# Seven products for eight pairs in GEMM2, in two groups, with a reordered convolution

## The chip, the core and the metric

One core of a Trainium2 chip runs the kernel. The metric is device time in microseconds. The kernel before was run three times: 1254.81, 1254.21 and 1253.92, median 1254.21. One more execution was profiled. Engine names as in the profile: PE is TensorE, PEld its weight loads, DVE VectorE, ACT ScalarE, POOL GpSimd, SP the queue that issues most DMAs.

## What is computed

With x = A_q (2048 x 1024) and xn its layer norm over the last axis, the output is x + A + B:

```python
# A: convolution branch
for t in range(ks):                       # ks = 4
    k_shift = k_shift + k_pad[:, t:t + S, :] * shift_k[:, ks - 1 - t]
kv = k_shift * v
y = irfft(rfft(kv, 2S) * rfft(ssm_k, 2S))[:S] + kv * ssm_D
A = xn * y
# B: feed-forward branch
h = silu(xn @ w1)                         # 2048 x 3584
B = h @ w2                                # 2048 x 1024
```

All is float32. The kernel forms each product of matrices from float16 parts (hi and lo of both operands, three matmuls: hi hi, hi lo, lo hi).

## The kernel before, in words

**Planner.** The program is written out once by a planner (`Order`, L118). Every strand of work is a generator (a stream) that yields either an operation with an engine and an expected cost, or a condition (a `Token` or a free buffer). The planner always emits the operation that could start first, less the stream's bias (`add(gen, bias)`). What it emits is each engine's queue, and a queue runs strictly in order on the chip. So a flag orders what is emitted; the real waits follow from data and buffers.

**GEMM1.** F = 3584 is 28 blocks of 128, which are 14 pairs. Pairs 0 and 1 partly run plain; the others take seven products instead of eight for a 2 x 2 blocking (`PRODUCTS`, L50): the factors of w1 and x are hi and lo splits of sums (`factors_w1`, `x_rows`, `more_sums`). `units` (L993) runs `P1, P7, P6, P2, P5, (next P1), P3, P4` per pair and row half `sp`; `evacuate` (L909) turns PSUM banks (tile ff) into h through SiLU.

**From h to GEMM2.** A pair that is not in `PAIRS` is split into hi and lo and stored plain (`blocks`, L871: one split of 1024 columns per pair and quarter). A pair in `PAIRS` = (8, 9, 10, 11) goes to `quad` (L828), which makes the seven left factors of GEMM2: splits of (A11, A12), A22, (S3, S1) and (S2, S4), and four sums, stored in the DRAM tiles `hsf`. `split` (L370) is always a ScalarE copy to hi and a VectorE subtraction (L352) to lo.

**GEMM2.** `feed_forward` (L1057) first runs the 20 plain blocks (`PLAIN`) as five chunks of four, for column half 1 (h = 0) and then half 0, over 16 row tiles; `result` stores each tile. Then `units2` (L1118) runs the seven products of the four pairs for eight tile quadruples u, each with four output tiles; `evacuate2` (L1184) adds two of them on VectorE (`v_stt`) and sends all to `out` by accumulating DMAs on POOL (`G`, L344). The last unit waits for the flag "conv out", reads one tile back and stores it plainly.

**Factors of w2.** `norms_w2` (L1304) fills eight places of 8 KB a partition (`places`, tile x in the profile, which held x in GEMM1). Plain chunks go to `W2PLACE`; the seven right factors and a float32 `hold` go to `FPLACE` as the chunks leave. Raw w2 comes through four half slots (wraw, w2n), in 36 loads for the seven products (`RAWS`, `load_w2`).

**Convolution.** Eight channel groups g, each a two-stage transform on VectorE with DFT matmuls on TensorE. Per group: `gate` (taps and product with v into sig), `signal_parts` (cm, transposes by DMA), `stage1` (DFT matmuls into ps banks; i = 0 gives a half, i = 1 adds the rest), `to_spec` (L1589: ScalarE copies twice the half into "diff" and the sum into "total", VectorE subtracts), `forward`, `product`, `inverse`, `result_parts` (splits into zh, zl), `stage1_inv` (L1753, into py banks), `gated` (multiplies with xg, writes to out). Quarters are taken in the order `TO` = (1, 3, 0, 2). Diffs of odd quarters lie in tmp, those of even ones in spec. The flag "taken" says that `result_parts` of the group before has read a quarter's slot. When GEMM1 has ended, `spare` (L1586) lets stage 1 use ff banks too. Conv outputs of groups 0 to 3 are plain stores on SP, those of 4 to 7 accumulate on POOL.

Of the kernel before, what the change touches and what calls it, by code (L numbers as in the profile page):

```python
# [20 lines left out]
P = 128  # L21
# [32 lines left out]
PAIRS = (8, 9, 10, 11)  # L54
UNITS = [[*range(2, NP)], [NP - 1, 0, 1, *range(2, NP - 1)]]
NQ = len(PAIRS)
# [7 lines left out]
RAWS = {"B11": [(0, 0)], "B21": [(1, 0)], "B22": [(1, 1)], "T1": [(0, 1), (0, 0)], "T2": [(0, 0)],  # L64
        "T3": [(1, 1), (0, 1)], "T4": [(1, 0)]}
# [235 lines left out]
def h3_ffn_kernel(ctx, tc, x, kp, vs, fs, shift, dskip, w1, w2, cfwd, cinv, out):  # L301
# [77 lines left out]
    hsf = [{p[0]: dram.tile([4, P, NQ, 2, P], F16, name=f"hsf{p[0]}{b}") for p in PRODUCTS.values()} for b in range(2)]  # L379
# [448 lines left out]
    def quad(i, sp):  # L828

        def factors(names, hf, toks=()):  # L830
# [4 lines left out]
            for f, name in enumerate(names):  # L835
                yield L(hsf[sp][name][:, :, PAIRS.index(i)].rearrange("q p h s -> p q (h s)"),
                        ht[:, 4 * f:4 * f + 4].rearrange("p q h s -> p q (h s)"))
                ttok.set()
# [18 lines left out]
    for sp in range(2):  # L857
        flag["quads", sp] = Token(NQ)

# [197 lines left out]
    def feed_forward():  # L1057
# [13 lines left out]
        for h in range(2):  # L1071
            for ts in TOGETHER[h]:
                pos = {}
                for c in range(NC):
                    for t in ts:
                        if c == 0:
                            yield ff.ready
                            pos[t] = ff.tile([P, W])
                        yield flag["h", h, t, c]
                        hx, htok = flag["h", h, t, c].what  # L1080
                        yield flag["w2", h, c]
                        wc, wtok = w2c[h, c]
                        yield from steps2(pos[t][0], hx, wc, c == 0, c == NC - 1)
                        htok.set()
                        if t == NT - 1:
                            wtok.set()
                        if c == NC - 1:
                            add(result(h, t, *pos[t]), EB)
        flag["last part"].set()
        yield from units2()  # L1090


    TOGETHER = ([range(3)] + [(t,) for t in range(3, NT)],
                [(t,) for t in range(NT - 3)] + [range(NT - 3, NT)])

    def steps2(po, hx, wc, first, last, more=False):
        for n in range(4):
            def mm(n=n):
# [3 lines left out]
                nc.tensor.matmul(po, hx[:, n, 1, :], wc[:, n, 0, :], start=False, stop=last and n == 3, **kw)  # L1102
# [15 lines left out]
    def units2():  # L1118

        def product2(n, u, o, first=False, cols=slice(0, W), end=True):  # L1120
            yield flag["h2", u, n]
            hx, htok = flag["h2", u, n].what
            yield flag["w2f", n]
            wc, wtok = w2f[n]
            yield from steps2(o[:, cols], hx, wc[:, :, :, cols], first, True, not first)
            if end:
                htok.set()
                if u == len(tiles2) - 1:
                    wtok.set()

        def start(u):
# [4 lines left out]
            add(evacuate2(u, one, made, seen), EB)  # L1136
# [3 lines left out]
        for u in range(len(tiles2)):  # L1140
# [23 lines left out]
            if u + 1 < len(tiles2):  # L1164
# [5 lines left out]
            if u + 1 < len(tiles2):  # L1170
# [6 lines left out]

    def at(u, r, h):

        sp, q = tiles2[u]  # L1180
        t = 4 * (2 * sp + r) + q
        return orr[t // T2, t % T2, :, h * W:(h + 1) * W]

    def evacuate2(u, one, made, seen):  # L1184

        last = u == len(tiles2) - 1
# [5 lines left out]
        def copied(src, tok, to):  # L1192
# [3 lines left out]
            yield G(to, o)  # L1196
# [16 lines left out]
        if not last:  # L1213
            yield made["P2"]
            add(copied(*one, at(u, 0, 0)), EB)
# [7 lines left out]
        if last:  # L1223
            yield made["P2"]
            add(copied(*one, at(u, 0, 0)), EB)
        yield G(at(u, 1, 1), d)
# [5 lines left out]
        add(copied(two, k2, at(u, 0, 1)), EB)  # L1232
        if not last:
# [3 lines left out]
            yield G(at(u, 1, 0), a)  # L1237
# [11 lines left out]
    for n in range(NT):  # L1249
        flag["conv row", n] = Token(NG // 2)  # L1250

    def columns(h):

        return slice((1 - h) * W, (2 - h) * W)

    def result(h, t, po, tok):
# [4 lines left out]
        to = orr[t // T2, t % T2, :, columns(h)]  # L1261
        if h == 0:
            yield L(to, o)
            flag["row", t].set()
        else:
            yield flag["conv row", t]
            yield G(to, o)
        otok.set()

    def load_h():  # L1270
        yield flag["factors"]
        for h in range(2):
            for c, t in [(c, t) for ts in TOGETHER[h] for c in range(NC) for t in ts]:
# [4 lines left out]
        for u, n in uses2():  # L1278
            sp, q = tiles2[u]
            yield wo.ready  # L1280
            flag["h2", u, n].what = o, _ = wo.tile([P, NQ, 2, P], F16)
            yield L(o, hsf[sp][PRODUCTS[n][0]][q])
            flag["h2", u, n].set()
# [20 lines left out]
    def norms_w2():  # L1304
# [17 lines left out]
        add(load_w2(), 0.05)  # L1322
        for h in range(2):
            for c in range(NC):
                r = places[W2PLACE[h][c]]
                yield r.ready
                if (h, c) == (0, 0):
                    yield flag["x", 1, "A22"]
                wc, wtok = w2c[h, c] = r.tile([P, 4, 2, W], F16)
                flag["w2", h, c].n = 2  # L1330
                for a in (0, 2):
# [586 lines left out]
```

## Time and profile before

| | us |
|---|---|
| median of the runs | 1254.21 |
| profiled execution, device time | 1252.18 |
| its span, first to last instruction | 1250.1 |
| PE busy | 1235.8 |
| DVE busy | 1108.4 |
| ACT busy | 779.5 |
| mean granted TensorE clock | 0.995 |

The span is what the profile's stretches and timelines are measured in; around it lie 2.1 us of the profiled execution. Matmuls overlap, so a busy PE says only that one was in flight; the distance from one start to the next is what a matmul takes. The same holds, less strongly, for DVE, whose instructions overlap by some 0.08 us at their ends. In rows of waits, "A <- B: 25.8, 20, 3.6" means that A was idle 25.8 us in total in 20 waits ended by B, the longest 3.6.

### The profile page before, as it was taken

To read this page: it belongs to the slowest core of one execution; us is meant where nothing else is said; L and a number is where in the kernel's file an instruction comes from. 1 tells how busy PE (TensorE), PEld (TensorE's weight loads), DVE (VectorE), ACT (ScalarE), POOL (GpSimd) and SP (SyncE) were. 2 spreads that over 40 slices of the span, in tenths; PEclk is the share of its full clock that TensorE was granted. 3 is DMA by queue.
4 is the path that set the end of the run, shared out by engine and by line. 5 is a ranking of instruction groups with operands and counts; after the bars stand their busy time and mean duration, and the time that the engine had idled before them with its cause. 6 is when DMAs were issued, how large, how long until landed. Compare 5 with 4: busy or idle time off the path is not lost.

```text
span 1250.1 us, 17015 instructions
## 1 busy us (share of the span) xinstructions
PE 1235.8 (99%) x6092; PEld 602.9 (48%) x6092; DVE 1108.4 (89%) x1252; ACT 779.5 (62%) x1361; POOL 83.3 (7%) x93
## 2 busy tenths in 40 slices
PE   9999999999999999999999999999999999899998
PEld 8544444444444544445444544544444444344444
DVE  7999987997999779998899799799889989987981
ACT  7768987886688886569653732753463374544342
POOL 0000000000000000000000000001031030113114
PEclk9999999999999999999999999999999999989999
DMA  9368889789899899769876566489487587958768
GB/s 367 101 231 273 309 308 337 230 252 253 231 339 304 242 312 301 216 193 316 298 241 186 148 195 176 130 285 255 118 201 186 140 193 212 241 104 128 163 129 110
DMA packets 267332, 279.82 MB, mean 224 GB/s; under 512 B 73200, under 2 KB 192240, under 8 KB 265968
## 3 DMA queue, kind: packets, MB, share of 16 engines
q1 hardware_dynamic: 251520, 262.22, 68.0%
q0 software_dynamic: 15728, 16.52, 10.2%
q8 instruction: 47, 0.77, 0.3%
q14 instruction: 37, 0.30, 0.1%
HBM read 175.66 MB, written 88.34 MB: 211 GB/s over the span
## 4 chain that ended last, share of the span: by engine, by line
PE 95%; DVE 3%; ACT 1%; DMA 1%; issue 0%; SPq 0%; ACTq 0%
PE ff L1101 14%; PE ff L1102 14%; PE ff L1100 14%; PE ff L957 14%; PE ff L958 14%; PE ff L959 14%; PE ps L1579 2%; PE ps L1580 2%; PE ps L1581 2%; PE py L1768 1%; PE py L1769 1%; PE py L1767 1%; PE ft L597 1%; DVE x L352 1%; DVE spec L349 1%
## 5 line engine op out<-in xcount | busy, mean ns | idle before, releaser
L1101 PE MATMUL ff<-x,wo 128*128 128x512 f16 x868 | 328.7, 379 | 4.6 <-DVE x L352 4.6
L1100 PE MATMUL ff<-x,wo 128*128 128x512 f16 x868 | 328.7, 379 | 2.2 <-ACT x L360 1.1
L1102 PE MATMUL ff<-x,wo 128*128 128x512 f16 x868 | 328.9, 379 | 0.0
L959 PE MATMUL ff<-x,wo 128*128 128x512 f16 (+1 forms) x808 | 302.8, 375 | 0.0
L958 PE MATMUL ff<-x,wo 128*128 128x512 f16 (+1 forms) x808 | 302.8, 375 | 0.0
L957 PE MATMUL ff<-x,wo 128*128 128x512 f16 (+1 forms) x808 | 302.7, 375 | 0.0
L349 DVE TENSOR_TENSOR spec<-spec 128x1024 f32<-128x1024 f32 (+2 forms) x232 | 259.6, 1146 | 2.0
L1102 PEld LDWEIGHTS <-wo 128*128 128x128 f16 x868 | 85.0, 98 | 107.2 <-issue 6.3
L1101 PEld LDWEIGHTS <-wo 128*128 128x128 f16 x868 | 85.0, 98 | 102.0 <-issue 4.0
L1100 PEld LDWEIGHTS <-wo 128*128 128x128 f16 x868 | 86.0, 99 | 99.2 <-issue 0.8
L959 PEld LDWEIGHTS <-wo 128*128 128x128 f16 x808 | 79.0, 98 | 92.1
L957 PEld LDWEIGHTS <-wo 128*128 128x128 f16 x808 | 80.5, 100 | 87.8
L958 PEld LDWEIGHTS <-wo 128*128 128x128 f16 x808 | 79.0, 98 | 88.1 <-issue 0.2
L349 DVE TENSOR_TENSOR tmp<-spec 128x2048 f32<-128x2048 f32 (+1 forms) x48 | 92.3, 1933 | 0.9
L352 DVE SCALAR_TENSOR_TENSOR ht<-hf,wsc,ht 128x1024 f16<-128x1024 f32 (+1 forms) x56 | 67.4, 1203 | 10.0 <-ACT ht L360 9.9
L352 DVE SCALAR_TENSOR_TENSOR wo<-raw,wsc,wo 128x1024 f16<-128x1024 f32 (+1 forms) x56 | 64.0, 1146 | 8.3 <-ACT wo L360 8.1
L360 ACT ACTIVATE spec<-spec 128x1024 bf16<-128x1024 f32 x32 | 33.8, 1055 | 60.3 <-DVE spec L349 60.3
L352 DVE SCALAR_TENSOR_TENSOR sig<-kin,taps,sig 128x1024 f32<-128x1024 f32 x48 | 61.5, 1280 | 11.2 <-ACT sig L360 11.1
L360 ACT ACTIVATE wo<-raw,wsc 128x1024 f16<-128x1024 f32 (+1 forms) x56 | 58.0, 1036 | 12.4 <-DVE raw L349 7.3
L346 POOL DMA_DIRECT2D out<-hf x44 | 38.3, 875 | 359.9 <-ACT hf L360 219.4
L360 ACT ACTIVATE ht<-hf,wsc 128x1024 f16<-128x1024 f32 (+1 forms) x56 | 60.9, 1087 | 2.0 <-DMA hsfA<-ht 0.3
L349 DVE TENSOR_TENSOR spec<-tmp 128x512 f32<-128x512 f32 (+1 forms) x80 | 60.8, 794 | 0.9
(187 smaller groups left out, 1712.7 us busy)
## 6 DMA issues: line engine op xcount, KB each, us to landing
wo<-hs SPq DMA_DIRECT2D x160, 256.0 KB, 3.4
hs<-ht SPq DMA_DIRECT2D x80, 256.0 KB, 4.3
raw<-in_w SPq DMA_DIRECT2D x28, 512.0 KB, 5.5
wraw<-in_w SPq DMA_DIRECT2D x24, 512.0 KB, 5.2
w2n<-in_w SPq DMA_DIRECT2D x24, 512.0 KB, 6.4
ws_T<-wo SPq DMA_DIRECT2D x22, 512.0 KB, 5.6
kin<-in_kp SPq DMA_DIRECT2D x16, 704.0 KB, 5.8
wo<-ws_T SPq DMA_DIRECT2D x22, 512.0 KB, 4.6
```

What stands on the lines that cost most here:

```text
L346: return Op("POOL", 1.1, 3.0, lambda: nc.gpsimd.dma_start(o, i, accum_op=ADD), [i], [o], m, 2.3 * n)
L349: return V(lambda: nc.vector.tensor_tensor(o, a, b, op=op), o, [a, b], **k)
L352: return V(lambda: nc.vector.scalar_tensor_tensor(o, a, s, b, op0=op0, op1=op1), o, [a, b] + ([] if isinstance(s, float) else [s]), **k)
L360: nc.scalar.activation(o, i, func, scale=scale, **kw)
L957: nc.tensor.matmul(o, w[:, 0, k], xf[:, :, k, 0], start=first and k == 0, stop=False, **kw)
L958: nc.tensor.matmul(o, w[:, 0, k], xf[:, :, k, 1], start=False, stop=False, **kw)
L959: nc.tensor.matmul(o, w[:, 1, k], xf[:, :, k, 0], start=False, stop=last and k == KH - 1, **kw)
L1100: nc.tensor.matmul(po, hx[:, n, 0, :], wc[:, n, 0, :], start=first and n == 0, stop=False, **kw)
L1101: nc.tensor.matmul(po, hx[:, n, 0, :], wc[:, n, 1, :], start=False, stop=False, **kw)
L1102: nc.tensor.matmul(po, hx[:, n, 1, :], wc[:, n, 0, :], start=False, stop=last and n == 3, **kw)
L1579: nc.tensor.matmul(o, cf[:, 0], h, start=i == 0, stop=False, **kw)
L1580: nc.tensor.matmul(o, cf[:, 0], l, start=False, stop=False, **kw)
```

## The change

Pairs 4 to 7 join the seven-product scheme of GEMM2, as a first group. The plain blocks fall from 20 to 12 (three chunks). The order is now: plain half 1, seven products of group 0, plain half 0, seven products of group 1.

```diff
-PAIRS = (8, 9, 10, 11)
+GROUPS = ((4, 5, 6, 7), (8, 9, 10, 11))
+PAIRS = sum(GROUPS, ())
+WHERE = {i: (k, a) for k, g in enumerate(GROUPS) for a, i in enumerate(g)}
-W2PLACE = [(2, 6, 4, 0, 3), (1, 5, 7, 2, 6)]
-FPLACE = (4, 0, 3, 1, 5, 7, 2, 6)
+W2PLACE = ((2, 6, 4), (0, 1, 5))
+FPLACE = ((0, 3, 1, 5, 7, 2, 6, 4), (3, 6, 7, 4, 2, 0, 1, 5))
...
-        flag["last part"].set()
-        yield from units2()
+            flag["seven", h].set()
+            yield from units2(h)
+            flag["plain", h + 1].set()
+    TOGETHER = [range(3)] + [(t,) for t in range(3, NT - 3)] + [range(NT - 3, NT)]
```

The factors of w2 are made per group from 20 loads instead of 36: each raw quarter is loaded once or twice and kept over two uses.

```diff
+    def seven_w2(g):
...
+        yield from room_for("P7")
+        for a in range(n):
+            b22, t22 = yield from next_w2()
+            b12, t12 = yield from next_w2()
+            yield v_tt(hold[:, a], b22, b12, SUB)
...
+        yield from room_for("P1")
+        for a in range(n):
+            b11, t11 = yield from next_w2()
+            split_of("P1", a, b11, t11)
+            yield flag["T3", g, a]
+            yield v_tt(hold[:, a], hold[:, a], b11, ADD)
...
+        yield from room_for("P6")
...
+        yield from room_for("P2")
...
+            b21, t21 = yield from next_w2()
...
+            split_of("P2", a, b21, flag["B21", g, a])
+        for a, (b21, _) in enumerate(raws2):
+            yield flag["B21", g, a]
+            yield v_tt(b21, b21, hold[:, a], SUB)
+        yield from room_for("P4")
...
+            b22, t22 = yield from next_w2()
...
+            yield flag["T2", g, a]
+            yield v_tt(hold[:, a], b22, hold[:, a], SUB)
+        yield from room_for("P5")
...
+        yield from room_for("P3")
```

All writes to `out` go through one rule: the first writer of a row tile and channel group stores plainly on SP, later ones accumulate on POOL; a result whose columns the convolution has partly written is cut in two.

```diff
+    def written(places_in, to, o):
+        new = [q not in first for q in places_in]
+        if new[0]:
...
+            yield L(to, o)
...
+        for q in places_in:
+            yield first[q]
+        yield G(to, o)
+    def put(t, h, o):
+        groups = range(h * NG // 2, (h + 1) * NG // 2)
+        there = sum((t, g) in first for g in groups)
+        for part in (groups[there:], groups[:there]):
...
```

In the convolution the squares of kf in `gate` are written to cm and stand ahead of its wait; that wait is now for the even quarters of the group before ("spec", g - 1, 0). Odd quarters copy and subtract before they wait for "taken", and may use py banks. The result parts of odd quarters go to slots 4 to 7 of the signal's half of spec, with the flag "z read" to guard them. The rows of x (`norm_rows`) get bias -1.0.

```diff
+                for a in range(2):
+                    yield cm_r.ready
+                    j, tok = cm_r.tile([P, T2 * P], BF16)
+                    yield a_act(j, kf[:, a].rearrange("p t w -> p (t w)"), AF.Square, total=ss[:, 2 + a:3 + a])
+                    tok.set()
                 if g > 0:
-                    yield flag["stage1", g - 1]
-                for a in range(2):
...
+                    yield flag["spec", g - 1, 0]
...
-                                yield lambda: ps_r.ready() or spare()
-                                ps, tok = (ps_r if ps_r.ready() else ff).tile([P, 2, 2 * P])
+                                yield lambda: bank_for(g, t) is not None
+                                ps, tok = bank_for(g, t).tile([P, 2, 2 * P])
...
+        def bank_for(g, t):
+            if ps_r.ready():
+                return ps_r
+            free = g == 0 or flag["taken", g - 1, t]()
+            if g > 0 and py_r.ready() and flag["un", g - 1]() and (free or t % 2):
+                return py_r
+            return ff if free and spare() else None
         def spare():
-            return flag["gemm1"]() and not flag["last part"]() and len(ff.free()) > 1
+            if not flag["gemm1"]() or len(ff.free()) < 2:
+                return False
+            return not flag["seven", 0]() or flag["plain", 1]() and not flag["seven", 1]()
...
-            if g > 0:
+            if g > 0 and t % 2 == 0:
                 yield flag["taken", g - 1, t]
+                yield flag["z read", g - 1, 3]
             yield a_act(diff, ps, AF.Copy, 2.0)
             seen.set()
             yield made
-            yield a_act(total, ps, AF.Copy)
-            yield v_tt(diff, diff, ps, SUB)
+            if t % 2:
+                yield v_tt(diff, diff, ps, SUB)
+                if g > 0:
+                    yield flag["taken", g - 1, t]
+                yield a_act(total, ps, AF.Copy)
+            else:
+                yield a_act(total, ps, AF.Copy)
+                yield v_tt(diff, diff, ps, SUB)
...
+            if g > 0:
+                yield flag["z read", g - 1, 1]
             yield flag["spec", g, 1]
...
+                    if t % 2:
+                        if t == 3:
+                            yield flag["inverse", g, 0]
+                        ipart[g, t] = [(half_word(sp[:, 0, AT[4 + n]]), flag["z read", g, t]) for n in ((1, 3), (0, 2))[t // 2]]
+                    else:
+                        ipart[g, t] = yield from parts_tile(more["zh"], more["zl"], (P, 2, 2 * 2 * P))
```

More of the change, by code (lines that the diff above doesn't have):

```diff
@@ L1322, in norms_w2 @@
         add(load_w2(), 0.05)
+        yield flag["x", 1, "A22"]
         for h in range(2):
[L1324 to L1331, printed above, removed]
[L1332 to L1334 removed]
```

261 lines of the change are left out of this document (137 added, 124 removed).

## The prediction

> **What bounds the kernel now.** I read the page first, then the stretches, then the chain.
>
> ```profile
> span 1250.1 us, 17015 instructions
> PE 1235.8 (99%) x6092; PEld 602.9 (48%) x6092; DVE 1108.4 (89%) x1252; ACT 779.5 (62%) x1361; POOL 83.3 (7%) x93
> ...
> PE 95%; DVE 3%; ACT 1%; DMA 1%; issue 0%; SPq 0%; ACTq 0%
> ```
>
> TensorE sets the end, and VectorE is at 89%. So work taken from TensorE pays only as far as VectorE keeps up. By stretches (length, then busy time of PE, PEld, DVE, ACT and POOL, clock, DMA share, GB/s):
>
> ```profile
> 100.00:250.00 150.00, 150.00 (x707) 69.26 (x706) 133.80 (x163) 124.63 (x188) 0.94 (x1) 1.00 0.86 289
> 250.00:650.00 400.00, 400.00 (x1920) 188.15 (x1918) 361.95 (x377) 295.93 (x496) 2.27 (x3) 1.00 0.90 271
> 650.00:1050.00 400.00, 399.95 (x1959) 191.89 (x1958) 366.25 (x364) 200.24 (x402) 32.14 (x33) 1.00 0.68 184
> 1050.00:1110.00 60.00, 53.79 (x233) 23.21 (x231) 56.67 (x64) 24.39 (x42) 6.02 (x7) 0.91 0.77 195
> 1110.00:1207.50 97.50, 97.50 (x478) 46.66 (x477) 86.22 (x87) 42.56 (x75) 25.30 (x27) 1.00 0.77 147
> 1225.00:1250.10 25.10, 20.53 (x107) 10.18 (x104) 3.07 (x5) 3.68 (x6) 9.53 (x10) 0.96 0.77 108
> ```
>
> TensorE is gapless but for one stretch, 1050 to 1110, and the tail. VectorE lies between 88% and 94% busy all along until 1207, and is then nearly done: the convolution lives on VectorE and ends only some 25 us ahead of the kernel. There are two clocks in this kernel: TensorE's queue, and VectorE's queue with the convolution at its end.
>
> What one matmul costs, and what the one stall costs, is in TensorE's timeline:
>
> ```profile
> 1073.59 0.38 PE L1102 MATMUL ff<-x,wo 128*128 128x512 f16 x1
> 1074.51 0.38 PE L1100 MATMUL ff<-x,wo 128*128 128x512 f16 x1 [0.54 <-ACT ff L360]
> ...
> 1087.45 0.38 PE L1100 MATMUL ff<-x,wo 128*128 128x512 f16 x1
> ...
> 1097.51 0.59 PE L1101 MATMUL ff<-x,wo 128*128 128x512 f16 x1 [1.78 <-DVE x L352]
> ...
> 1101.25 0.38 PE L1101 MATMUL ff<-x,wo 128*128 128x512 f16 x1
> ```
>
> From 1074.51 to 1087.45 there are 60 steps: 12.94 / 60 = 0.2157 us for each 512-column matmul (the 0.38 is overlapped). From 1073.59 to 1101.25 there are 80 steps, worth 17.3 us, in 27.7 us: this stall, on the w2 factors (tile x) of the seven products, loses 10.4 us. Part of that is the clock:
>
> ```profile
> 1092.00:1096.00 4.00, 1.95 (x4) 0.50 0.55 118
> PE ff L1101 <- DVE x L352: 4.6, 4, 1.8
> ```
>
> The granted clock was 0.50 there though no single wait passed 1.8 us. [...]
>
> **TensorE's side of the change.** Plain GEMM2 goes from 20 to 12 F-blocks: 16 row tiles x 2 halves x 8 blocks x 3 matmuls = 768 fewer. A second group of seven products adds 8 tiles x 7 x 4 x 3 = 672. Net 96 x 0.2157 = 20.7 us less. GEMM1, the convolution's matmuls and their number are as before. The floor by TensorE is 1250.1 - 20.7 = 1229.4, or 1219.0 if the 10.4 us stall goes too.
>
> **VectorE's side.** Prices are steps from start to start, from VectorE's timeline:
>
> ```profile
> 404.50 1.28 DVE L352 SCALAR_TENSOR_TENSOR ht<-hf,wsc,ht 128x1024 f16<-128x1024 f32 x1
> 405.69 0.74 DVE L352 SCALAR_TENSOR_TENSOR cm<-sig,csc,cm 128x512 f16<-128x512 f32 x1
> ...
> 1085.72 0.75 DVE L352 SCALAR_TENSOR_TENSOR hf<-ff,invc,hf 128x512 f32<-128x512 f32 x1
> 1086.38 0.74 DVE L352 SCALAR_TENSOR_TENSOR cm<-sig,csc,cm 128x512 f16<-128x512 f32 x1
> ...
> 1088.31 0.69 DVE L349 TENSOR_TENSOR x<-wraw,x 128x512 f32<-128x512 f32 x1
> 1088.91 0.69 DVE L349 TENSOR_TENSOR x<-w2n,x 128x512 f32<-128x512 f32 x1
> ```
>
> A split of 1024 is 1.19, one of 512 is 0.66, a sum of 512 is 0.60.
> Factors of h: each of the four added pairs, in each of two row halves, trades two 1024 splits for three and one of 512, and makes four sums: 1.19 + 0.66 + 2.40 = 4.25, times 8 = 34.0.
> Factors of w2: eight 1024 splits go (-9.5); one more group brings 28 splits of 512 (18.5) and 16 sums (9.6): 18.6. The sums per group are 16 as before; the 20 loads instead of 36 save transfers, not VectorE time.
> Evacuation: eight more units with two scaled adds each: 16 x 0.66 = 10.6.
> Together 63.2 us more. ScalarE takes the matching copies and has 38% free overall. Nothing in the convolution's own arithmetic goes away; it is only reordered.
>
> So what would VectorE's queue make of it? The end of the convolution and what must follow it:
>
> ```profile
> 1224.18 0.69 DVE L349 TENSOR_TENSOR ht<-py,ht 128x512 f32<-128x512 f32 x1 [0.72 <-ACT py L360]
> 1237.61 0.69 ACT L360 ACTIVATE ht<-ff,invc 128x512 f32<-128x512 f32 x1 [4.49 <-PE ff L1102]
> 1246.14 0.48 DVE L352 SCALAR_TENSOR_TENSOR hf<-ff,invc,hf 128x256 f32<-128x256 f32 x1 [0.91 <-PE ff L1102]
> out<-hf SPq DMA_DIRECT2D x2, 128.0 KB, 2.6
> ```
>
> After the last gated product (done 1224.9) the last unit needs a copy (0.7), P3 and P4 (24 x 0.2157 = 5.2), a scaled add (0.5) and a store (2.6); with 1 us of issue that is 10, so 1235 against 1250.1: the convolution may end 15 us later before it decides. The end by VectorE is therefore 1250.1 + 63.2 - 15 - R = 1298.3 - R, where R is how much of its present waiting VectorE fills. R decides the case. Its waits, with total, times and longest:
>
> ```profile
> DVE tmp L349 <- ACT spec L360: 25.8, 20, 3.6
> DVE ht L352 <- ACT ht L360: 18.6, 13, 7.7
> DVE spec L349 <- ACT spec L360: 18.4, 10, 4.6
> DVE sig L352 <- ACT sig L360: 11.1, 7, 6.3
> DVE zl L352 <- ACT zh L360: 10.6, 8, 3.3
> DVE wo L352 <- ACT wo L360: 8.1, 9, 2.8
> DVE x L352 <- ACT x L360: 4.9, 7, 1.6
> DVE hf L349 <- PE ff L959: 3.5, 5, 1.5
> ```
>
> *Early odd quarters*: the difference of an odd quarter goes to tmp, which is free once the group's product is done, so copy, second matmuls and subtraction run under the previous group's inverse, in py banks too; only the total waits until the slot is taken. This removes the wait of tmp, nearly all: 25 of 25.8 (bounds 13 and 25.8, since the total's four copies still come late). What is late next is the even quarters: their diffs now also wait until the third quarter's parts, put into left slots, are read by TensorE ("z read"). Behind that wait stand the total, the subtraction and the forward transform. But the forward transform's odd part can start some 5 us sooner, so I take half of the 18.4: 9 (0 to 18).
> *Squares into cm*, ahead of the wait for stage 1: two of them leave the front of each gate,
>
> ```profile
> L360 ACT ACTIVATE sig<-kf 128x1024 bf16<-128x1024 f32 x16 | 16.7, 1051 | 0.0
> ```
>
> 2.1 us of ScalarE: 8 of 11.1 (4 to 11). cm is one buffer, free from the transposes by then.
> *Result parts in left slots*: no wait for zh and zl: 6 of 10.6 (0 to 10.6).
> *Waits in GEMM1* (ht without its 7.7 in the tail, wo, hf: 22.5): the added sums fill half, 11 (5 to 22).
> *w2 factors*: 3 of 4.9 (0 to 4.9).
> R = 25 + 9 + 8 + 6 + 11 + 3 = 62, between 22 and 93. End 1236.3, later than TensorE's floor, so VectorE's queue decides and some of TensorE's gain is given back as small waits.
>
> **What I cost at nothing.** The out writes grow by one accumulating result per unit:
>
> ```profile
> q0 software_dynamic: 15728, 16.52, 10.2%
> out<-hf POOLq DMA_DIRECT2D x44, 256.0 KB, 4.3
> ```
>
> 32 more of 256 KB, some cut in two where the convolution has written only part of the columns. POOL is at 7%, so its issue is hidden; a result behind a late one keeps an hf slot 4.3 us longer. Transfers in GEMM1 grow: 56 factor stores of 256 KB for 32 of plain h, +6 MB in a stretch whose engines are 0.90 busy; at 271 GB/s 23 us of transfer against some 40 us free. If that cover were gone, stores would hold ht and delay the splits of h by those 23 us at most. SP's loads of w2 stand in one queue with the loads of h; per group 20 come where 36 came, so that queue is shorter.
>
> **Rivals.**
> *B, TensorE stays the bound*: R above 69. For it: VectorE's long full stretches. Against it: 1108.4 + 63.2 = 1171.6 in 1229 is 95% over a span that holds a start and a tail in which VectorE idles anyway; no stretch above reaches it. 1219.0 to 1229.4, taken as 1226 in the span.
> *C, ScalarE bounds the change of groups* (the slower side). At such a change:
>
> ```profile
> 992.40:1016.20 23.80, 23.80 (x135) 13.05 (x134) 18.73 (x22) 21.22 (x43) 8.80 (x8) 1.00 0.63 103
> ```
>
> ScalarE is busy 21.2 of 23.8 us, VectorE 18.7. If the early copies only move work within a full ScalarE queue, the waits of spec, zl and x gain nothing and that of sig the low bound: R = 25 + 0 + 4 + 0 + 10 + 0 = 39, end 1259.3. It decides below R = 48.
> *D, the stall comes twice*: each group has three factors (P4, P5, P3) whose places come free only as the plain chunks end. Time: 1229.4 + 10.4 = 1239.8. Against: the last three row tiles run chunk by chunk (9 matmul groups of 2.59), so the first such place is free 15.5 us ahead of the products, and P3 is first used six products later, 15.5 us; in these 31 us VectorE owes 12 splits and 4 sums, 10.3 us.
> *E, no early quarters*: the banks are held, ps by the first and py by stage 1 of the inverse, so that the copies stay where they were. R loses 25 and 8: 29, end 1269.
>
> **How the numbers follow.** The profiled execution took 1252.2, 2.1 around its span, and the median of the runs is 2.0 above it: add 4.1. Forecast A: 1240.4, chance 0.52, with its own range 1232 to 1251 (R from 70 to 51). B 1230, 0.16. C 1263, 0.15. D 1244, 0.12. E 1273, 0.05. No change within 0.2% (2.5 us, about what a measurement of this kernel can tell) means 1251.7 to 1256.7. Faster: 0.46 of A, 0.16 of B, 0.07 of D: 0.69. Same: 0.05, 0.02 of D, 0.01 of C: 0.08. Slower: the rest, 0.23. Range 1226 to 1263, which leaves out the low end of B, half of C, and E.
>
> **What would show it.** Right: about 5996 matmuls, 63 us more VectorE time (some 1171), the wait "tmp <- ACT spec" nearly gone, the VectorE share near 95%, the convolution's last product within 15 us of the end. Wrong: VectorE's waits as before (C, E), a clock of 0.50 in two places in GEMM2 (D), or TensorE full until the tail (B). The forecast falls if the waits move to spec and zl instead of going, or if the last convolution output is not near the end.

## The result, and the profile after

The changed kernel took 1273.7 us (median of 4 runs, 1270.71 to 1276.67), beside 1254.07 us for the kernel before: ratio 1.0159, 95% interval 1.0135 to 1.0183. It is slower by 1.6%. The forecast was 1240.4 and the range 1226 to 1263, so both the direction and the range were wrong.

The page of the changed kernel (device time of the profiled execution 1276.67 us): span, busy times, and the shares of the chain that ended last.

```profile
span 1274.9 us, 17136 instructions
...
PE 1227.6 (96%) x5996; PEld 596.1 (47%) x5996; DVE 1169.4 (92%) x1352; ACT 823.0 (65%) x1437; POOL 115.1 (9%) x129
...
PE 53%; DVE 25%; issue 8%; DMA 7%; ACT 6%; POOL 1%; SPq 0%; DVEq 0%; ACTq 0%; POOLq 0%
```

Matmuls fell to the 5996 that were forecast and VectorE rose by 61.0 us to 1169.4 (63.2 forecast). The chain that was 95% TensorE is now 53% TensorE; VectorE, ScalarE and DMA hold 38% of it: the bound moved, as forecast. What did not come is the rest.

The cleanest account is a ledger of VectorE's queue up to the convolution's last gated product: that instant, VectorE's busy and idle time up to it, and the tail from it to the end of the span. The windows that give it, of the kernel before (same columns as in the prediction):

```profile
0.00:1224.90 1224.90, 1215.15 (x5987) 592.60 (x5988) 1105.33 (x1247) 775.70 (x1356) 73.66 (x84) 1.00 0.79 226
620.00:1224.90 604.90, 598.64 (x2913) 285.70 (x2911) 547.99 (x548) 292.41 (x569) 69.74 (x74) 0.99 0.71 181
100.00:620.00 520.00, 520.00 (x2485) 243.67 (x2484) 465.96 (x513) 405.81 (x652) 3.22 (x4) 1.00 0.89 276
```

and of the changed kernel, with the stretch of the old stall:

```profile
0.00:1260.70 1260.70, 1219.38 (x5960) 591.97 (x5961) 1167.10 (x1348) 820.98 (x1434) 109.15 (x124) 0.99 0.82 228
620.00:1260.70 640.70, 621.95 (x3015) 296.23 (x3014) 597.69 (x617) 347.87 (x672) 105.24 (x114) 0.99 0.78 192
100.00:620.00 520.00, 500.91 (x2355) 232.61 (x2354) 477.89 (x545) 395.50 (x628) 3.22 (x4) 0.98 0.90 271
1050.00:1110.00 60.00, 59.45 (x301) 29.36 (x300) 54.14 (x55) 41.68 (x80) 14.84 (x15) 1.00 0.80 191
```

Up to the convolution's end VectorE does 1167.10 - 1105.33 = 61.8 us more. Its idle time fell from 1224.9 - 1105.33 = 119.6 to 1260.7 - 1167.10 = 93.6: 26.0 us were filled, where the forecast had R = 62. The convolution therefore ended 35.8 us later, the tail gave back 25.2 - 14.2 = 11.0, and 35.8 - 11.0 = 24.8 is the growth of the span, 1250.1 to 1274.9. (The medians differ by 19.6: the profiled execution of the changed kernel is 3.0 above its median, that of the kernel before 1.9 below.) By stretches, idle went from 54.0 to 42.1 in 100 to 620 (mostly GEMM1) and from 56.9 to 43.0 behind it.

The stall on the w2 factors is gone: TensorE is busy 59.45 of 60 us in 1050 to 1110, where it was 53.79. But it lost time elsewhere. Summed over the steps of its timeline after 70 us, beyond 0.2157 us for 512 columns, it loses 61.7 us against 16.4 before: some 28 in GEMM1, 15 in small waits of GEMM2, 18.5 around and behind the convolution's end. That is 45.3 lost against the 20.7 that the removed matmuls save, and 45.3 - 20.7 = 24.6 is the growth once more: both ledgers close.

VectorE's waits in the changed kernel (total, times, longest):

```profile
DVE spec L349 <- ACT spec L360: 16.3, 10, 3.8
...
DVE ht L349 <- ACT py L360: 9.6, 7, 2.6
...
DVE spec L349 <- PE py L1858: 4.2, 4, 1.5
DVE spec L352 <- ACT spec L360: 4.2, 4, 2.0
...
DVE tmp L349 <- PE ps L1640: 3.8, 1, 3.8
DVE xg L349 <- ACT py L360: 3.5, 3, 1.5
...
DVE spec L349 <- PE ff L1102: 2.6, 1, 2.6
DVE zl L352 <- ACT zh L360: 2.5, 6, 0.8
DVE ht L349 <- ACT ff L360: 1.8, 1, 1.8
DVE tmp L349 <- ACT hf L360: 1.3, 1, 1.3
...
DVE sig L352 <- ACT sig L360: 0.8, 1, 0.8
...
DVE tmp L349 <- ACT spec L360: 0.7, 1, 0.7
```

and two rows of the kernel before that the prediction did not list:

```profile
DVE ht L349 <- ACT py L360: 2.2, 2, 1.5
DVE xg L349 <- ACT py L360: 1.5, 1, 1.5
```

The wait of tmp, 25.8 before, is down to single waits of 3.8, 1.3 and 0.7, and that of sig from 11.1 to 0.8. But the gated products (ht and xg, L349) now wait 9.6 + 3.5 + 1.8 = 14.9 instead of 3.7. The differences of the even quarters wait 16.3 + 2.6 = 18.9, no less than the 18.4 before. The 4.2 us that end with PE py L1858 are new: there the first sums of the forward transform (spec from tmp, 128x1024) wait until the inverse's matmuls have read the result parts in the left slots, which is what the flag "z read" guards. Of the 10.6 of zl there remain 2.5 + 4.2 (the odd result parts now lie in spec).

In GEMM1 the added work delays TensorE. Its timeline around one stall:

```profile
287.29 0.58 PE L959 MATMUL ff<-x,wo 128*128 128x512 f16 x1 [4.39 <-DVE hf L349]
...
291.93 0.38 PE L961 MATMUL ff<-x,wo 128*128 128x512 f16 x1
...
339.79 0.38 PE L959 MATMUL ff<-x,wo 128*128 128x512 f16 x1 [1.70 <-DVE hf L349]
```

and VectorE's ahead of it:

```profile
282.19 0.69 DVE L349 TENSOR_TENSOR x<-x 128x512 f32<-128x512 f32 x1
282.96 1.28 DVE L352 SCALAR_TENSOR_TENSOR ht<-hf,wsc,ht 128x1024 f16<-128x1024 f32 x1
284.16 1.28 DVE L352 SCALAR_TENSOR_TENSOR wo<-raw,wsc,wo 128x1024 f16<-128x1024 f32 x1
285.36 1.27 DVE L352 SCALAR_TENSOR_TENSOR ht<-x,wsc,ht 128x1024 f16<-128x1024 f32 x1
286.55 0.68 DVE L349 TENSOR_TENSOR hf<-ff,hf 128x512 f32<-128x512 f32 x1
```

The add that frees TensorE's bank (hf<-ff,hf at 286.55) does not wait for anything itself; VectorE comes to it late, out of a queue without a gap. The sums and splits right ahead of it are not the added ones: this is the eighth quad of the row half, that of pair 11, which made them before too. In the kernel before it was the fourth quad, and the same last sum and add stood here:

```profile
267.44 0.69 DVE L349 TENSOR_TENSOR x<-x 128x512 f32<-128x512 f32 x1
...
271.64 0.68 DVE L349 TENSOR_TENSOR hf<-ff,hf 128x512 f32<-128x512 f32 x1
```

With four quads added ahead of it the add comes 14.9 us later, and TensorE, which has no stall there in the kernel before, waits 4.39 us and then runs 11 steps in 4.64 us, at half speed (0.42 from start to start). So the 34 us of added VectorE work in GEMM1 did not slip into gaps alone: they lengthened GEMM1. In 100 to 620 TensorE was busy all 520.00 us before and 500.91 now.

### The profile page after: what moved, and what is told of

It is laid out like the page before. It is cut to its first block, busy times and chain, and to the rows that moved or that the text cites. A ratio compares the mean times of both kernels' runs of the same rounds, so it can differ in the third digit from the quotient of the medians.

```text
span 1274.9 us, 17136 instructions
## 1 busy us (share of the span) xinstructions
PE 1227.6 (96%) x5996; PEld 596.1 (47%) x5996; DVE 1169.4 (92%) x1352; ACT 823.0 (65%) x1437; POOL 115.1 (9%) x129
## 4 chain that ended last, share of the span: by engine, by line
PE 53%; DVE 25%; issue 8%; DMA 7%; ACT 6%; POOL 1%; SPq 0%; DVEq 0%; ACTq 0%; POOLq 0%
PE ff L1100 8%; PE ff L1102 8%; PE ff L1101 8%; PE ff L959 7%; PE ff L960 7%; PE ff L961 7%; DVE spec L349 6%; DVE ht L352 3%; DVE tmp L349 3%; DVE x L352 2%; DVE sig L352 2%; DMA hsfA<-ht 2%; DVE hf L349 2%; DMA wraw<-in_w 2%; DVE spec L352 2%
## 5 line engine op out<-in xcount | busy, mean ns | idle before, releaser
L1100 PE MATMUL ff<-x,wo 128*128 128x512 f16 x836 | 317.5, 380 | 9.9 <-ACT hf L360 4.7
L959 PE MATMUL ff<-x,wo 128*128 128x512 f16 (+1 forms) x808 | 305.9, 379 | 18.4 <-DVE hf L349 12.4
L1101 PE MATMUL ff<-x,wo 128*128 128x512 f16 x836 | 317.2, 379 | 0.0
L1102 PE MATMUL ff<-x,wo 128*128 128x512 f16 x836 | 317.2, 379 | 0.0
L960 PE MATMUL ff<-x,wo 128*128 128x512 f16 (+1 forms) x808 | 305.9, 379 | 0.0
L961 PE MATMUL ff<-x,wo 128*128 128x512 f16 (+1 forms) x808 | 305.7, 378 | 0.0
L349 DVE TENSOR_TENSOR spec<-spec 128x1024 f32<-128x1024 f32 (+2 forms) x232 | 260.1, 1146 | 1.9
L1101 PEld LDWEIGHTS <-wo 128*128 128x128 f16 x836 | 82.0, 98 | 107.3 <-issue 13.1
L960 PEld LDWEIGHTS <-wo 128*128 128x128 f16 x808 | 79.5, 98 | 109.9 <-issue 23.3
L1102 PEld LDWEIGHTS <-wo 128*128 128x128 f16 x836 | 82.0, 98 | 98.7 <-issue 1.4
L1100 PEld LDWEIGHTS <-wo 128*128 128x128 f16 x836 | 82.7, 99 | 96.3 <-issue 1.4
L961 PEld LDWEIGHTS <-wo 128*128 128x128 f16 x808 | 79.6, 98 | 94.1 <-issue 3.5
L959 PEld LDWEIGHTS <-wo 128*128 128x128 f16 x808 | 80.9, 100 | 90.1 <-issue 3.1
L346 POOL DMA_DIRECT2D out<-hf x76 | 67.4, 891 | 409.0 <-ACT hf L360 176.5
L349 DVE TENSOR_TENSOR tmp<-spec 128x2048 f32<-128x2048 f32 (+1 forms) x48 | 92.7, 1932 | 0.8
L360 ACT ACTIVATE hf<-ff,invc 128x512 f32<-128x512 f32 x61 | 41.4, 679 | 52.8 <-PE ff L1102 48.0
L346 POOL DMA_DIRECT2D kf<-in_dskip x8 | 7.0, 878 | 685.9 <-DMA kf<-in_fs 254.7
L352 DVE SCALAR_TENSOR_TENSOR ht<-hf,wsc,ht 128x1024 f16<-128x1024 f32 (+1 forms) x56 | 63.0, 1126 | 3.0 <-ACT ht L360 2.8
L349 DVE TENSOR_TENSOR spec<-tmp 128x512 f32<-128x512 f32 (+1 forms) x80 | 60.9, 793 | 5.0 <-PE py L1858 4.2
L360 ACT ACTIVATE ht<-hf,wsc 128x1024 f16<-128x1024 f32 (+1 forms) x56 | 57.2, 1023 | 8.1 <-DMA hsfA<-ht 2.6
```

The source lines that it names most:

```text
L346: return Op("POOL", 1.1, 3.0, lambda: nc.gpsimd.dma_start(o, i, accum_op=ADD), [i], [o], m, 2.3 * n)
L349: return V(lambda: nc.vector.tensor_tensor(o, a, b, op=op), o, [a, b], **k)
L352: return V(lambda: nc.vector.scalar_tensor_tensor(o, a, s, b, op0=op0, op1=op1), o, [a, b] + ([] if isinstance(s, float) else [s]), **k)
L360: nc.scalar.activation(o, i, func, scale=scale, **kw)
L959: nc.tensor.matmul(o, w[:, 0, k], xf[:, :, k, 0], start=first and k == 0, stop=False, **kw)
L960: nc.tensor.matmul(o, w[:, 0, k], xf[:, :, k, 1], start=False, stop=False, **kw)
```

## The experiments

Theory V: VectorE's queue up to the convolution's last product sets the end, and too little of its idle time was recovered. Rivals: TensorE's stalls in GEMM1 set it; one of the convolution's edits itself does harm; the w2 factors do. All rows of the ledger, with the time of the runs (the kernel before took 1252.87 to 1254.43 in the runs beside them):

| kernel | convolution ends | busy to it | idle to it | tail | median us | ratio to before, interval |
|---|---|---|---|---|---|---|
| before | 1224.9 | 1105.3 | 119.6 | 25.2 | 1254.07 | |
| after | 1260.7 | 1167.1 | 93.6 | 14.2 | 1273.70 | 1.0159 (1.0135 to 1.0183) |
| e1_noconv | 1288.4 | 1168.4 | 120.0 | 18.1 | 1310.17 | 1.0465 (1.0447 to 1.0482) |
| e2_conv4 | 1184.3 | 1099.7 | 84.6 | 76.8 | 1264.31 | 1.0097 (1.0082 to 1.0113) |
| e3_w20 | 1221.9 | 1105.6 | 116.3 | 20.0 | 1243.45 | 0.9927 (0.9912 to 0.9941) |
| e4_conv4_w20 | 1193.1 | 1101.8 | 91.3 | 62.4 | 1258.32 | 1.0046 (1.0031 to 1.0061) |
| e5_nosum_h | 1246.9 | 1148.4 | 98.5 | 14.8 | 1262.78 | 1.0079 (1.0051 to 1.0107) |
| e6_nosum_w2 | 1241.2 | 1152.3 | 88.9 | 13.4 | 1258.34 | 1.0037 (1.0024 to 1.0050) |
| e7_pool_h | 1278.8 | 1175.2 | 103.6 | 18.6 | 1299.92 | 1.0371 (1.0356 to 1.0386) |
| e8_odd | 1251.9 | 1167.5 | 84.4 | 13.8 | 1268.20 | 1.0120 (1.0102 to 1.0137) |
| e9_squares | 1273.1 | 1168.2 | 104.9 | 19.4 | 1294.97 | 1.0333 (1.0309 to 1.0357) |
| e10_slots | 1282.7 | 1168.5 | 114.2 | 14.7 | 1299.40 | 1.0367 (1.0350 to 1.0384) |
| e11_no_slots | 1246.5 | 1165.9 | 80.6 | 19.7 | 1270.00 | 1.0132 (1.0112 to 1.0151) |
| e12_w20_squares | 1211.2 | 1104.5 | 106.7 | 31.7 | 1243.91 | 0.9927 (0.9914 to 0.9941) |

**Eight pairs without the convolution's edits (e1_noconv).** Against the changed kernel, all edits in the convolution are undone, the bias of the rows of x among them:

```diff
+                if g > 0:
+                    yield flag["stage1", g - 1]
...
-                    yield cm_r.ready
-                    j, tok = cm_r.tile([P, T2 * P], BF16)
+                    j = acc[:, a].bitcast(BF16)[:, 0:TQ].rearrange("p t w -> p (t w)")
...
-                                yield lambda: bank_for(g, t) is not None
+                                yield lambda: ps_r.ready() or spare()
...
-            if t % 2:
-                yield v_tt(diff, diff, ps, SUB)
-                if g > 0:
-                    yield flag["taken", g - 1, t]
-                yield a_act(total, ps, AF.Copy)
```

> The change with the edits in the convolution undone (early odd quarters, squares in cm, left slots, py banks, bias of the rows); eight pairs and the new w2 factors stay. Theory V (VectorE's queue up to the convolution's last product sets the end, work plus waits): the waits tmp<-ACT (25.8 before, 5.8 after), sig (11.1, 0.8) and zl come back, less the new waits of the gated products (about 11) and of the even quarters (5): 18 to 26 us later, 1292 to 1300 us. Rival C (the reordered convolution itself costs, since ScalarE bounds a change of groups): not later than 1274.

Its windows:

```profile
100.00:620.00 520.00, 499.62 (x2351) 232.14 (x2349) 474.39 (x540) 393.28 (x622) 3.23 (x4) 0.98 0.89 275
620.00:1288.40 668.40, 621.76 (x3020) 297.37 (x3019) 602.55 (x622) 351.35 (x677) 107.30 (x115) 0.97 0.75 180
```

and VectorE's waits:

```profile
DVE spec L349 <- ACT spec L360: 28.6, 12, 5.5
DVE tmp L349 <- ACT spec L360: 19.1, 16, 3.8
...
DVE sig L352 <- ACT sig L360: 10.7, 5, 5.3
...
DVE ht L349 <- ACT py L360: 8.4, 6, 3.3
...
DVE zl L352 <- ACT zh L360: 6.7, 7, 1.8
...
DVE xg L349 <- ACT py L360: 1.5, 2, 0.9
```

The time, 1310.17, is 10 us later than theory V had put it. This run splits R. VectorE has 63.1 us more to do and is as idle as before in all (120.0 for 119.6): the added work fills nothing, net. In 100 to 620 it does fill 54.0 - 45.6 = 8.4, but behind it 668.4 - 602.55 = 65.9 are idle where 56.9 were. The rows say where: the even quarters wait 28.6 instead of 18.4 and the gated products 9.9 instead of 3.7, while tmp fell from 25.8 to 19.1. TensorE's stalls in GEMM1 are there without the convolution's edits (499.62 us busy of 520), so they come with the added pairs. All 26.4 us that the changed kernel recovers come from the convolution's edits, for which the forecast had 48; they are worth 36 us of time by the medians, 31.6 between the profiled executions.

**Four pairs with the convolution's edits (e2_conv4), with the new w2 factors (e3_w20), with both (e4_conv4_w20).** e2 puts the convolution's edits alone into the kernel before, the diff above the other way round. e3 takes the order of `seven_w2` into the kernel before:

```diff
-RAWS = {"B11": [(0, 0)], "B21": [(1, 0)], "B22": [(1, 1)], "T1": [(0, 1), (0, 0)], "T2": [(0, 0)],
-        "T3": [(1, 1), (0, 1)], "T4": [(1, 0)]}
+RAWS = {"T3": [(1, 1), (0, 1)], "T2": [(0, 0)], "B21": [(1, 0)], "B22": [(1, 1)]}
...
+        for i, of, uses in [(i, *q) for q in (("T3", 1), ("T2", 2), ("B21", 1), ("B22", 1)) for i in PAIRS]:
...
+        yield from room_for("P7")
```

e4 has both edits.

> The kernel before, four pairs, with the edits in the convolution alone. V: the convolution's last product comes some 20 us earlier than 1224 of the span, TensorE then sets the end alone, and the stall on the w2 factors stays: 1248 to 1254 us. Rival C: the last product comes no earlier, and the time is 1254 or more.

> The kernel before, four pairs, with the w2 factors made in the new order from 20 loads alone. If the stall of 10.4 us on these factors came from their order and their 36 loads: it shrinks below 4, and the end falls until the convolution's tail holds it (last product 1225 of the span plus 10 to 14): 1242 to 1248 us. If it came from VectorE being full: the stall stays and the time is 1252 to 1256.

> Both on four pairs: the convolution's edits and the new w2 factors, without the second group. V: neither the convolution nor the factors hold TensorE any more, so the time is the one before less the stall: 1240 to 1246 us, below both kernels. If V is wrong and the convolution's edits bring nothing: 1244 to 1254.

In e2 the convolution ended 40.6 us earlier, with 35.0 us less idle time, and the kernel took 11 us longer, where V had it at or below the kernel before. With four pairs TensorE sets the end, and the convolution's edits put new waits into its queue. TensorE's waits in e2:

```profile
PE ff L1798 <- ACT spec L360: 6.8, 9, 1.2
...
PE ps L1582 <- ACT spec L360: 1.5, 2, 1.2
PE ff L1798 <- DVE spec L349: 1.3, 1, 1.3
```

It loses 27.6 us after 70 us, where the kernel before loses 16.4: matmuls of the inverse (L1798, which read the result parts in the left slots of spec) and of stage 1 (L1582) now stand at the head of TensorE's queue before ScalarE or VectorE has their operand, and with them stands GEMM2. The rows on tile x, the stall on the w2 factors, are gone in e2 although it keeps the old 36 loads (57.55 of 60 us busy in 1050 to 1110), so its new losses are larger than the difference of 11.2 shows. e3 is the opposite. The same stretch that held the stall, in e3:

```profile
1050.00:1110.00 60.00, 59.43 (x279) 27.08 (x277) 59.41 (x69) 29.11 (x54) 7.97 (x10) 1.00 0.73 168
```

TensorE loses 8.1 us instead of 16.4, and the time is 1243.45: this part alone beats both kernels by the stall that it removes. Together (e4) 11.4 slower and 9.4 faster would make 2.0 slower; 5.4 were measured (V had expected 1240 to 1246), so the edits do not quite add either; that each alone removes the same stall is one reason why.

**Less work for VectorE (e5_nosum_h, e6_nosum_w2).** e5 leaves out the four sums of the h factors for pairs 4 to 7; e6 leaves out the 24 sums of the w2 factors that work on kept quarters:

```diff
+        if i in GROUPS[1]:
             yield v_tt(v, z, v, ADD)
             yield v_tt(z, x, z, SUB)
...
-            yield v_tt(hold[:, a], hold[:, a], b11, ADD)
...
-            yield v_tt(b21, b21, hold[:, a], SUB)
...
-            yield v_tt(hold[:, a], b22, hold[:, a], SUB)
```

> The change without the four sums of the left factors of h for the added pairs 4 to 7, which are left out; their splits, stores and buffers stay. That is 32 sums of 0.60 = 19.2 us less on VectorE in GEMM1. V: the end comes about 19 us earlier, 1252 to 1260 us. Rival G (TensorE loses time in GEMM1 because the added factors hold slots of hf and ht through splits and stores, and that sets the end): TensorE's losses in GEMM1 of some 28 us stay and the time is 1268 or more.

> The change without 24 of the 32 sums of the w2 factors (those that make T2, T4 and T1), which are left out; loads, splits and places stay. 14.4 us less on VectorE, all of it after GEMM1. V: 10 to 15 us earlier, 1259 to 1264 us, with TensorE's losses in GEMM1 as they were. Rival G: nothing of GEMM1 changes, 1272 or more.

The windows up to the convolution's end, first of e5:

```profile
0.00:1246.90 1246.90, 1212.92 (x5960) 590.51 (x5961) 1148.41 (x1316) 821.65 (x1434) 108.03 (x122) 0.99 0.83 231
```

then of e6:

```profile
0.00:1241.20 1241.20, 1213.05 (x5960) 590.75 (x5961) 1152.31 (x1324) 819.53 (x1434) 108.39 (x122) 1.00 0.84 232
```

e5 takes 18.7 us from VectorE in GEMM1, and the time falls by 10.9, which lies between V and rival G; TensorE's losses in GEMM1 halve, from some 28 to some 14. The stall behind pair 11 stays (a wait of 5.65 us at 279.73), so the sums are not all of its cause. e6 takes 14.8 us from VectorE in GEMM2, and the time falls by 15.4, about as V had it, with GEMM1's losses still some 22. So a microsecond of VectorE's work behind GEMM1 is worth a microsecond of time, and one in GEMM1 a little over half: stalls of GEMM1 alone do not set the end, VectorE's queue does.

**The 64 sums of h on GpSimd (e7_pool_h).**

```diff
+    def p_tt(o, a, b, op):
+        return Op("POOL", 1.6, 0.3, lambda: nc.gpsimd.tensor_tensor(o, a, b, op=op), [a, b], [o], 0.15)
...
-        yield v_tt(v, z, v, ADD)
-        yield v_tt(z, x, z, SUB)
+        yield p_tt(v, z, v, ADD)
+        yield p_tt(z, x, z, SUB)
```

> The change with the 64 sums of the left factors of h (eight pairs, two halves, four each) on GpSimd instead of VectorE. It takes 38 us from VectorE. V: the convolution ends early enough that TensorE sets the end, 1236 to 1250 us, below both kernels. Rival G: the sums take longer there and the slots of hf are held longer, so TensorE loses more in GEMM1: 1270 or more.

1299.92: slower by 26 us than the changed kernel, though 64 x 0.60 = 38 us left VectorE's queue. Its busy time up to the convolution's end even rose, to 1175.2. GpSimd's sums, by groups (busy and mean ns, then idle before):

```profile
L352 POOL TENSOR_TENSOR hf<-x,hf 128x512 f32<-128x512 f32 x16 | 32.1, 2005 | 1.3
```

and VectorE beside them, in the timeline of both engines:

```profile
157.39 1.28 DVE L355 SCALAR_TENSOR_TENSOR wo<-raw,wsc,wo 128x1024 f16<-128x1024 f32 x1
...
159.41 1.65 POOL L352 TENSOR_TENSOR hf<-hf 128x512 f32<-128x512 f32 x1 [17.22 <-DVE ht L355]
159.85 2.30 DVE L355 SCALAR_TENSOR_TENSOR wo<-raw,wsc,wo 128x1024 f16<-128x1024 f32 x1
```

The same split takes 1.28 us alone and 2.30 beside a sum on GpSimd; in the whole run the 56 splits of this group (wo<-raw,wsc,wo, 1024 and 512 columns) take 1.287 on average, in the changed kernel 1.145. TensorE loses 84.9 us instead of 61.7. As a test of V this run says nothing, since it did not relieve VectorE.

**The convolution's edits one by one (e8_odd, e9_squares, e10_slots), and all but the slots (e11_no_slots).** Eight pairs each, on top of e1. e8 has the early odd quarters with py banks, e9 the squares in cm with the gate's later flag, e10 the left slots with "z read"; e11 is the changed kernel without the last. The bias of the rows of x, -1.0 in the changed kernel and in e11, is 0.0 in e1, e8, e9 and e10; no run changes it alone. The lines of the odd quarters and of the squares are in the diff of e1, taken the other way; those of the slots, as e11 removes them:

```diff
-                yield flag["z read", g - 1, 3]
...
-            if g > 0:
-                yield flag["z read", g - 1, 1]
...
-                    if t % 2:
-                        if t == 3:
-                            yield flag["inverse", g, 0]
-                        ipart[g, t] = [(half_word(sp[:, 0, AT[4 + n]]), flag["z read", g, t]) for n in ((1, 3), (0, 2))[t // 2]]
-                    else:
-                        ipart[g, t] = yield from parts_tile(more["zh"], more["zl"], (P, 2, 2 * 2 * P))
+                    (hi, htok), (lo, ltok) = ipart[g, t] = yield from parts_tile(more["zh"], more["zl"], (P, 2, 2 * 2 * P))
```

> Eight pairs and the new w2 factors, and of the convolution's edits only the early odd quarters with the py banks. If the edits add up as the prediction's terms did: VectorE's idle time up to the convolution's last product (120 us without the edits, 94 with all) falls by about 20, the wait tmp<-ACT (19.1) goes, and the time is 1290 to 1296 us. Rival: the early quarters only move the wait to spec and the gated products: idle falls by less than 8, 1302 us or more.

> Eight pairs and the new w2 factors, and of the convolution's edits only the squares in cm, with gate's other flag. If the terms add: idle falls by 8, the wait sig<-ACT (10.7) goes: 1300 to 1304 us. Rival, the gate is only put behind the even quarters: 1308 or more.

> Eight pairs and the new w2 factors, and of the convolution's edits only the result parts of odd quarters in left slots, with their z read flags. If the terms add: zl<-ACT (6.7) goes and idle falls by 4 to 6: 1303 to 1308 us. Rival: the z read waits of the even quarters eat it: 1310 or more.

> The change without the left slots and their z read flags; all other edits stay. If the z read waits are what made the wait of the even quarters and of the gated products: both shrink and the time is below the change's, 1262 to 1270 us. If the left slots bring what the prediction said: 4 to 8 us above it, 1278 to 1284.

Idle time recovered against e1: odd quarters 35.6, squares 15.1, slots 5.8; the sum is 56.5, but all together give 26.4. Alone, the first two bring about twice what was expected of them (20 and 8), and the third what was expected (4 to 6). Why they do not add shows in the waits of e8, where the odd quarters alone are early:

```profile
DVE spec L349 <- ACT spec L360: 15.5, 13, 3.8
...
DVE zl L352 <- ACT zh L360: 3.7, 3, 2.8
...
DVE sig L352 <- ACT sig L360: 1.7, 2, 0.9
```

The waits of zl and sig, which the other two edits were to take, have already shrunk (6.7 and 10.7 in e1; sig waits 3.8 more there for a DMA). The odd quarters alone (1268.2) beat the changed kernel (1273.7; the ranges of the runs, 1267.45 to 1269.8 and 1270.71 to 1276.67, do not touch). Without the slots (e11) 13.0 us less are idle than in the changed kernel. So the slots, which help a little alone, give nothing and rather take when the odd quarters are early; whether the bias of the rows takes part in this is not shown. In time that is 3.7 us by the medians, and the two intervals overlap: the tail of e11 is 5.5 us longer, and the profiled execution of the changed kernel is 3.0 above its median while that of e11 is 2.0 below. The forecast suspected the flag "z read", which holds the even quarters. In e10 it may be seen there: their row is 37.2, where e1 has 28.6. In the changed kernel it shows at its other place, the 4.2 us of the forward transform (<- PE py L1858), a row that e11 does not have; the even quarters wait no less in e11 (21.5). How much of the 13.0 the flag makes is not shown. In e11's tail (ScalarE's timeline) the last copies wait for a slot of ht, which a store of the convolution still holds:

```profile
1252.92 1.27 ACT L360 ACTIVATE ht<-ff,invc 128x512 f32<-128x512 f32 x2 [7.09 <-DMA out<-ht]
```

**Squares alone on four pairs with the new factors (e12_w20_squares).** Against e3:

```diff
-                if g > 0:
-                    yield flag["stage1", g - 1]
...
-                    j = acc[:, a].bitcast(BF16)[:, 0:TQ].rearrange("p t w -> p (t w)")
+                    yield cm_r.ready
+                    j, tok = cm_r.tile([P, T2 * P], BF16)
...
+                if g > 0:
+                    yield flag["spec", g - 1, 0]
```

> Four pairs in seven products, the w2 factors from 20 loads (1243.5 us alone), and of the convolution's edits only the squares into cm with the later wait of the gates. Theory T (with four pairs TensorE's queue sets the end, so waits of VectorE that are filled bring nothing; what made four pairs slower with all the convolution's edits, 1264.3, was the early quarters, whose copies push the copies that TensorE waits for): the convolution ends 5 to 15 us sooner than 1221.9, the tail behind it grows by as much, and the time stays within 3 us of 1243.5. Rival X (any reorder of the gates disturbs TensorE's queue): new waits of stage-1 and inverse matmuls on ACT spec, over 5 us more lost by TensorE after 70 us than the 8.1 of the w2 edit alone, time 1249 or more. Rival W (VectorE still sets the end at four pairs): the time falls by 5 us or more, to 1238 or less.

Theory T holds: the convolution ends 10.7 us sooner, the tail is 11.7 longer, and the time is the same (1243.91 for 1243.45; TensorE loses 9.7 and 8.1). So the squares are not what harmed e2. With four pairs TensorE's queue is the bound, and recovered waits of VectorE are worth nothing.

## Why the prediction was wrong, point by point

- **TensorE's floor**: the 5996 matmuls are as forecast, and that the w2 stall would come twice (rival D) fell: the new order of the factors removes it (e3: 8.3 us less lost).
- **VectorE's added work**: right. 63.2 forecast, 61.8 measured up to the convolution's end; 32 sums of h at 0.60 are 19.2, measured 18.7 (e5); 24 sums of w2 are 14.4, measured 14.8 (e6). The 44 + 32 = 76 out writes of GpSimd are also what the profile counts in that group, and nothing shows them on the path.
- **The end by VectorE = 1298.3 - R**: the mechanism was right (chain, e5, e6). **The term that failed is R: 62 forecast, 26 measured.** It decided, since the forecast itself put the break-even at 48.
- **R's fill by the added work** (11 in GEMM1, 3 in w2): 8.4 came in the stretch of GEMM1, and 9.0 more were idle behind it, so nothing in all (e1). The forecast let the added work fall into gaps. In GEMM1 it also pushed back the adds that free TensorE's banks (row at 286.55), and some 28 us of TensorE stalls came with it, which none of the rivals had.
- **R's edits of the convolution** (25 + 9 + 8 + 6 = 48): 26.4 came (e1 to after). By the rows of the waits in these two kernels, tmp lost 19.1 - 5.8 = 13.3 where 25 were forecast, the even quarters 28.6 - 18.9 = 9.7 (9), sig 9.9 (8) and the result parts 9.2 - 6.7 = 2.5 (6; the 9.2 are 6.7 and two waits of 1.3 and 1.2). Against that the forward transform gained 4.2 behind "z read" and the gated products 14.9 - 9.9 = 5.0, neither of which the forecast had. Together that is 26.2 of the 26.4. The largest error among these is the term of tmp: it was priced at the wait of the kernel before, 25.8, of which the added work left 19.1 and the edit left 5.8. So the 36 between 62 and 26 are made up: 11.7 too much for tmp, 14 for the fill that did not come, 9.2 of new waits and 3.5 for the result parts, less 2.6 that the even quarters and sig gave beyond their terms, is 35.8. The forecast's own condition, that it falls if the waits move to spec and zl instead of going, was met only in part: new waits came at the forward transform and the gated products.
- **The slack of the tail**: 15 forecast, 11.0 measured. In the changed kernel's timeline the last copy waits for a slot of ht behind the convolution's own store, and TensorE, idle for 4.10 us, starts P3 at half clock (0.50 granted in 1262 to 1266):

```profile
1261.52 0.69 ACT L360 ACTIVATE ht<-ff,invc 128x512 f32<-128x512 f32 x1 [1.50 <-DMA out<-ht]
1262.25 0.59 PE L1100 MATMUL ff<-x,wo 128*128 128x512 f16 x1 [4.10 <-ACT ht L360]
```

- **The rivals**: B (TensorE stays the bound) fell. C had the right side and R = 39 by a busy ScalarE; ScalarE is busy 823.0 of 1274.9 us and was not shown to bound anything, so its mechanism stays untested (in windows of 24 us at four changes of groups, from 836, 965, 1052 and 1160, ScalarE is busy 14.4 to 21.5 us). E gave 1273, which is the measured time, but by a mechanism that did not happen: the early quarters came, and the wait of tmp went.
- **The range**: R had bounds of 22 and 93, and the measured 26 lies within them. The range's upper end of 1263 corresponds to R = 39; it cut off what the bounds allowed, because the terms were taken as independent. That 26 lies within the bounds is partly luck: the added work filled nothing in all, where at least 5 were forecast, and the 9.2 of new waits had no term; the even quarters and sig made up for it.

Why the added work lengthens the waits of the even quarters and of the gated products (e1), and why exactly the three edits overlap as they do, was not settled further: the convolution's steps form one chain across VectorE, ScalarE and TensorE, and it is argued, not shown, that this chain's own length is what remains when one wait of it is taken out.

## What to carry to other kernels

Idle time of VectorE's queue was not a store here that added work or removed waits drew on one by one: added work changed the waits that an edit was to remove (tmp, 25.8 to 19.1), two edits worked on the same wait (zl, 6.7 to 3.7 by the odd quarters alone), and new waits came further down the chain (9.2 at the forward transform and the gated products). Of the 48 forecast 26 came, so half of the sum was a closer guess than all of it. Before work is moved from the engine at 99% to the one at 89%, look at what the second engine owes the first (bank-freeing adds, operands): here such a debt, the add at 286.55, came 14.9 us later behind the new work. And try the parts alone: of this change one part, the new order of the w2 factors, gains 0.7% alone (0.9927, 0.9912 to 0.9941), and it was hidden in a whole that lost 1.6%.

## What the runs showed of the hardware

**VectorE beside sums on GpSimd.** In e7 a split (wo, 128x1024) took 2.30 us beside a sum on GpSimd and 1.28 alone, and GpSimd's sums took 2.0 us on average in the group shown (hf<-x,hf), where VectorE needs 0.68 in the changed kernel. With the 64 sums on GpSimd, VectorE was busier up to the convolution's end than with them in its own queue (1175.2 for 1167.1). Why a split takes longer beside such a sum was not shown.

**The clock behind a wait.** In the changed kernel a wait of 4.39 us was followed by 11 steps in 4.64 us (287.29 to 291.93), 2.3 us more than 11 x 0.2157; a wait of 1.70 us at 339.79 was not, and the clock stayed full there:

```profile
287.00:291.00 4.00, 3.71 (x9) 1.28 (x9) 2.43 (x6) 2.30 (x2) 0.00 (x0) 0.50 0.92 179
339.00:343.00 4.00, 3.21 (x15) 1.46 (x15) 4.00 (x5) 2.42 (x4) 0.00 (x0) 1.00 0.23 69
```

Other waits in the changed kernel's trace go the same way: the clock granted in the 4 us behind the waits of 3.70 us (259.26), 4.38 (603.84) and 4.10 (1262.25) was 0.50, and behind a wait of 2.07 us (924.13 to 926.40) it was 1.00. In the stall of the kernel before it was 0.50 too (1092 to 1096), where no wait passed 1.78 us but several stood close together. So the 4.39 us of the one wait in GEMM1 cost, beside the 1.70 of the other, not 2.7 us more but, by an estimate from these two waits, some 5.0 (2.7 + 2.3).
